# Two tiles' transposes moved up among the products, by 6 and 7 matmul pairs, one evacuation on VectorE during the Gelu table load, one norm behind the first products

## Chip, cores, metric

The kernel runs on one core of a Trainium2 chip. The metric is device time in microseconds (us) of one execution.

## The reference, cut to what matters

Input `x` is 2048 x 448 in bf16. It is layer-normed once, and the result `xn` feeds an attention branch and a gated feed-forward branch:

```python
xn = _layernorm(x, axis=-1)
s  = attention(xn, k_cache, v_cache, wq, wo)                    # 16 heads, window of 512 keys
g  = silu((gelu(xn @ w_gate) * (xn @ w_up)) @ w_down)           # F = 1792
return x + s * g
```

Only the first 14 us matter here: the layer norm of the first four tiles of 128 rows (tiles 0 to 3), their transposition to `xnT`, and the first products `xn @ w_gate`, `xn @ w_up`.

## The kernel before

A tile is normalized on VectorE (`ln_first`: statistics, then a square root on ScalarE; `ln_second`: reciprocal, then the norm itself). For tiles 0 to 3, TensorE (PE) transposes it into a PSUM bank pair (`ln_tp_pe`, "T0" to "T3"), and ScalarE copies ("evacuates") it to `xnT`. Later tiles are transposed by DMA. In the traces each engine's operations appear in the order of the program (ScalarE's before, for instance: the evacuations of T1, T2 and T3 at 7.54, 9.36 and 10.65 us, then the table load at 11.27).

```python
def ln_tp_pe(t, parts):
    ...
            K.op("pe", fn, ...)                      # 8 transposes of 64x128 into PSUM
    for i, b in parts:
        ...
        act(xnT[:, ks, t * P:(t + 1) * P]..., tp[:, ks, :, :], ACT.Copy, b_ps[b:b + 2], ...)   # ScalarE

def warm(n, b):                                      # n matmuls of 256 columns on zeros
    ...
```

`gu_group(units, banks, (a, b), phases)` issues the products of several output units with columns of tiles a to b. It goes through the units in passes: phase 0 has 4 pairs of 64-row matmuls per unit, phase 1 has 3 pairs. One pass over the HEAD, three units, is 12 or 9 pairs. `(0, 0)` and `(0, 1)` are the two halves of phase 0, 6 pairs each over the HEAD. The head of the program, in order:

```python
warm(20, 2)
ln_first(0); ln_first(1); ln_second(0)
ln_tp_pe(0, ((0, 6), (1, 4)))
warm(3, 2)
ln_second(1, "act")
HEAD, PH = (0, 1, 2), (0, 2, 4)
T = ((None, 6),)
ln_first(2)
gu_group(HEAD, PH, (0, 1), ((0, 0), (0, 1)))         # products with T0
ln_tp_pe(1, T)
ln_first(3); ln_second(2); ln_second(3)
ln_a(); ln_a(); ln_b(); ln_b()                       # statistics, then norms, of tiles 4 and 5
gu_group(HEAD, PH, (0, 1), (1,))
gu_group(HEAD, PH, (1, 2), (0,))                     # products with T1
gu_group(HEAD[:1], PH[:1], (1, 2), (1,))
ln_tp_pe(2, T)
gu_group(HEAD[1:], PH[1:], (1, 2), (1,))
gu_group(HEAD[:1], PH[:1], (2, 3), (0,))             # products with T2
ln_tp_pe(3, T)
act(tmp[:, 1, 0:1], nhalf[:, :], ACT.Gelu_apprx_tanh, ...)   # makes ScalarE load the Gelu table
gu_group(HEAD[1:], PH[1:], (2, 3), (0,))
gu_group(HEAD, PH, (2, 3), (1,))
gu_group(HEAD[:2], PH[:2], (3, 4))                   # products with T3
for ph in range(2):
    gu_group((3,), (6,), None, (ph,))                # first products of 512 columns
    gu_group(HEAD[2:], PH[2:], (3, 4), (ph,))
```

These loads of weights and of `x` are all issued from the start on, on SyncE's queue, without waiting for any other operation:

```python
load_x("sp", 4, 2)
for i in (1, 2):                                     # second and third block of w_gate, w_up
    load_w("sp", i, 0); load_w("sp", i, 1); load_wr("sp", i, 0); load_wr("sp", i, 1)
load_x("sp", 6, 2)
load_w("sp", 3, 0); load_w("sp", 3, 1)               # fourth block
load_x("sp", 8, 4)
```

The softmax here doesn't subtract the row's maximum and nothing guards it: scores larger than these inputs give would overflow.

## Time and profile before

| | kernel before |
|---|---|
| time, median of the first 3 runs | 557.43 us (557.25 to 557.52) |
| span of the profiled execution | 555.7 us |
| PE busy in it | 550.3 us |
| head, 0 to 13.4 us: PE busy | 11.58 us |

From the page of the profile before, the busy time of the engines and the chain that ended last:

```profile
span 555.7 us, 9787 instructions
...
PE 550.3 (99%) x3653; PEld 260.6 (47%) x3653; DVE 317.2 (57%) x816; ACT 274.4 (49%) x728; POOL 32.7 (6%) x64
...
PE 98%; DMA 1%; ACT 0%; DVE 0%; issue 0%
```

PE is the bound: it is busy for 99% of the span and makes up 98% of the chain. From the windows view of the same kernel (busy us of each engine in a stretch, instructions in brackets):

```profile
core 0: us, PE busy (x) PEld busy (x) DVE busy (x) ACT busy (x) POOL busy (x), PEclk, DMA share, GB/s
0.00:13.40 13.40, 11.58 (x225) 8.77 (x225) 8.41 (x31) 7.15 (x16) 2.24 (x10) 1.00 0.92 298
13.40:60.00 46.60, 46.60 (x398) 21.60 (x394) 31.15 (x70) 16.74 (x29) 8.87 (x22) 1.00 0.44 90
60.00:545.00 485.00, 484.83 (x2969) 224.82 (x2966) 274.84 (x711) 250.52 (x684) 21.57 (x33) 1.00 0.47 101
```

PE has nothing to lose from 13.4 us on (46.60 of 46.60), and 1.8 us idle before that. From PE's timeline of the kernel before (start, duration, line, operation, output and inputs, count, idle time before it and what ended it):

```profile
5.56 0.40 PE L420 MATMUL bank<-ident,xn 64*128 64x64 bf16 x8
...
7.22 0.28 PE L420 MATMUL bank<-ident,xn 64*128 64x64 bf16 x8
...
8.19 0.34 PE L327 MATMUL bank<-xnT,wgu 64*128 64x128 bf16 x6 [0.19 <-ACT xnT L321]
...
9.04 0.28 PE L420 MATMUL bank<-ident,xn 64*128 64x64 bf16 x8
...
10.10 0.34 PE L327 MATMUL bank<-xnT,wgu 64*128 64x128 bf16 x6 [0.45 <-ACT xnT L321]
...
10.32 0.30 PE L420 MATMUL bank<-ident,xn 64*128 64x64 bf16 x8
...
13.16 0.35 PE L327 MATMUL bank<-xnT,wgu 64*128 64x128 bf16 x6
13.33 0.24 PE L327 MATMUL bank<-xnT,wgur 64*128 64x128 bf16 x2
```

T1's transposes start at 7.22, and T1's first products at 8.19 wait for ScalarE. T2's start at 9.04, and its products at 10.10 wait again. An idle time in brackets counts from the modelled end of the matmul before; counted from start to start, less the 56 ns that a pair of 128-column matmuls takes, the two stalls are 0.35 and 0.61 us. ScalarE's timeline of the kernel before shows why:

```profile
7.54 0.60 ACT L321 ACTIVATE xnT<-bank 128x512 bf16<-128x512 bf16 x1 [0.46 <-PE bank L420]
...
9.36 0.60 ACT L321 ACTIVATE xnT<-bank 128x512 bf16<-128x512 bf16 x1 [1.04 <-PE bank L420]
10.65 0.60 ACT L321 ACTIVATE xnT<-bank 128x512 bf16<-128x512 bf16 x1 [0.70 <-PE bank L420]
11.27 1.28 ACT L321 ACT_TABLE_LOAD   x1
...
12.67 1.06 ACT L321 ACTIVATE gl<-bank 128x512 bf16<-128x512 f32 x2
```

These are the evacuations of T1, T2 and T3, the Gelu table load, and the first Gelu. PE waits for the ends of the first two. The table load comes only after all three.

### The profile page before, as it was taken

What the parts mean: (1) busy time and instruction counts of PE and PEld (TensorE: products, weight loads), DVE (VectorE), ACT (ScalarE), POOL (GpSimd) and SP (SyncE); (2) the same over time, 40 slices, a digit from 0 to 9 for tenths busy, and PEclk for the clock granted to TensorE, in tenths of its full rate; (3) what the DMA queues carried; (4) which work ended last, traced back from release to release, by engine and by line L of the source; (5) the groups of instructions that cost most, each with busy time, mean ns of one, the idle gap of its engine ahead of it and who ended that gap; (6) DMA issues with size and microseconds to landing.
All of it is one profiled execution on the core that took longest, in us unless ns stands there. A gap on an engine that the chain in (4) does not pass through costs nothing.

```text
span 555.7 us, 9787 instructions
## 1 busy us (share of the span) xinstructions
PE 550.3 (99%) x3653; PEld 260.6 (47%) x3653; DVE 317.2 (57%) x816; ACT 274.4 (49%) x728; POOL 32.7 (6%) x64
## 2 busy tenths in 40 slices
PE   8999999999999999999999999999999999999997
PEld 6444444444544444454444445544444454444455
DVE  6783534443385786515858753286785525858722
ACT  5432324353485784504758751085784504758600
POOL 1120830000000000000000000000000000000000
PEclk9999999999999999999999999999999999999999
DMA  9660799403175374313706703176364313807701
GB/s 300 105 164 9 204 292 313 71 1 39 38 132 98 76 139 91 76 35 89 153 20 152 152 20 75 34 140 105 77 151 77 77 34 90 153 20 152 153 8 34
DMA packets 163599, 57.63 MB, mean 104 GB/s; under 512 B 151456, under 2 KB 160672, under 8 KB 163552
## 3 DMA queue, kind: packets, MB, share of 16 engines
q1 hardware_dynamic: 159488, 45.16, 39.6%
q0 software_dynamic: 3296, 11.27, 6.4%
q8 instruction: 29, 0.48, 0.4%
q10 hardware_dynamic: 768, 0.57, 0.3%
q14 instruction: 18, 0.15, 0.1%
HBM read 17.92 MB, written 1.84 MB: 36 GB/s over the span
## 4 chain that ended last, share of the span: by engine, by line
PE 98%; DMA 1%; ACT 0%; DVE 0%; issue 0%
PE bank L327 97%; PE bank L435 1%; DMA pT<-pn 1%; ACT xnT L321 0%; PE bank L420 0%; DVE tmp L668 0%; DVE ofin L671 0%; DVE gl L357 0%; DVE epst L358 0%
## 5 line engine op out<-in xcount | busy, mean ns | idle before, releaser
L629 ACT ACTIVATE p<-bank 128x512 f32<-128x512 f32 x256 | 149.4, 597 | 102.4 <-PE bank L327 102.0
L633 DVE TENSOR_SCALAR pn<-p,rden 128x512 bf16<-128x512 f32 x256 | 124.4, 486 | 16.7 <-DMA pT<-pn 7.9
L327 PE MATMUL bank<-kT,qT 128*128 128x512 bf16 x512 | 121.0, 379 | 0.0
L327 PE MATMUL bank<-pT,va 128*128 128x512 bf16 x512 | 120.8, 379 | 0.2 <-DMA pT<-pn 0.2
L327 PE MATMUL bank<-wo,oT 128*128 128x448 bf16 (+2 forms) x544 | 97.8, 341 | 0.0
L327 PE MATMUL bank<-xnT,wq 64*128 64x512 bf16 x768 | 94.7, 376 | 0.0
L327 PE MATMUL bank<-xnT,wgu 64*128 64x512 bf16 (+1 forms) x780 | 83.4, 347 | 0.6 <-ACT xnT L321 0.6
L327 PEld LDWEIGHTS bank<-pT,va 128*128 128x128 bf16 x512 | 50.0, 98 | 60.8 <-DMA pT<-pn 0.8
L327 PEld LDWEIGHTS bank<-kT,qT 128*128 128x128 bf16 x512 | 49.4, 98 | 61.7 <-issue 3.4
L327 PEld LDWEIGHTS bank<-wo,oT 128*128 128x128 bf16 x544 | 52.0, 98 | 45.5
L615 DVE CAST qT<-bank 128x512 bf16<-128x512 f32 x64 | 42.9, 692 | 48.7 <-PE bank L327 48.7
L321 ACT ACTIVATE qT<-bank 128x512 bf16<-128x512 f32 x64 | 38.2, 597 | 62.1 <-PE bank L327 60.5
L327 PEld LDWEIGHTS bank<-xnT,wq 64*128 64x128 bf16 x768 | 36.8, 94 | 46.8 <-ACT p L629 2.5
L484 DVE TENSOR_TENSOR actT<-bank,gl 128x512 bf16<-128x512 f32 x56 | 37.8, 690 | 34.0 <-PE bank L327 26.7
L321 ACT ACTIVATE gl<-bank 128x512 bf16<-128x512 f32 x56 | 33.2, 597 | 48.0 <-PE bank L327 44.8
L327 PEld LDWEIGHTS bank<-xnT,wgu 64*128 64x128 bf16 x780 | 35.3, 94 | 39.0 <-issue 0.7
L632 DVE RECIPROCAL rden<-rsum 128x1 f32<-128x1 f32 x256 | 40.4, 158 | 22.0 <-ACT p L629 22.0
L629 ACT ACTIVATION_READ_ACCUMULATOR p<-bank 128x1 f32 x256 | 52.8, 206 | 0.0
L668 DVE SCALAR_TENSOR_TENSOR tmp<-bank,g 128x448 f32<-128x448 f32 (+2 forms) x17 | 10.1, 597 | 72.5 <-PE bank L327 72.5
L652 DVE CAST oT<-bank 128x512 bf16<-128x512 f32 x64 | 43.8, 684 | 6.9 <-PE bank L327 6.9
L327 PE MATMUL bank<-wd,actT 128*128 128x448 bf16 x224 | 43.0, 353 | 0.0
L321 ACT ACTIVATE oT<-bank 128x512 bf16<-128x512 f32 x64 | 39.2, 613 | 7.0 <-PE bank L327 7.0
(38 smaller groups left out, 185.1 us busy)
## 6 DMA issues: line engine op xcount, KB each, us to landing
wo<-in_A_wo_dram POOLq DMA_DIRECT2D x4, 896.0 KB, 18.0
wq<-in_A_wq_dram POOLq DMA_DIRECT2D x2, 1536.0 KB, 9.7
va<-in_A_v_cache_dram POOLq DMA_DIRECT2D x8, 256.0 KB, 12.7
pT<-pn SPq DMA_TRANSPOSE x128, 2.8
xr<-in_A_x_dram POOLq DMA_DIRECT2D x16, 112.0 KB, 2.3
out_dram<-ofin SPq DMA_DIRECT2D x15, 112.0 KB, 1.7
wd<-in_B_w_down_dram SPq DMA_DIRECT2D x1, 1568.0 KB, 7.3
x<-in_A_x_dram SPq DMA_DIRECT2D x2, 448.0 KB, 6.7
```

The lines of the kernel that those rows point to most:

```text
L321: K.op("act", lambda e, o=o, i=i: e.activation(o, i, func, scale=scale), reads, writes)
L327: ins = e.matmul(o, lhsT=l, rhs=r, start=st, stop=sp)
L435: ins = e.matmul(bank[b][:, 0:256], lhsT=gl[:, 0, 0:P], rhs=gl[:, 0, 0:256], start=True, stop=True)
L484: K.op("dve", lambda e: e.tensor_tensor(actT[:, c % 2, f, :], bank[b + 1], gl[:, s, :], ALU.mult), (b_ps[b + 1], b_gl[s]), (b_actT[c % 2][ ...
L615: K.op("dve", lambda v, s=s, b=b: v.tensor_copy(qT[:, s, 1, :], bank[b + 1]), (b_ps[b + 1],), (b_qT[s][1],))
L629: K.op("act", lambda e, b=b, r=r, z=z: e.activation(p32[:, z, :], bank[b], ACT.Exp, scale=att_scale, accum_out=rsum[:, r:r + 1]), (b_ps[b] ...
L632: K.op("dve", lambda e, r=r: e.reciprocal(rden[:, r:r + 1], rsum[:, r:r + 1]), (b_rsum[r],), (b_rden[r],))
L633: K.op("dve", lambda e, r=r, z=z, y=y, t=t4 % 2: e.tensor_scalar(pn[:, y, t, :], p32[:, z, :], rden[:, r:r + 1], None, op0=ALU.mult), (b_p ...
L652: K.op("dve", lambda v, i=i, b=b: v.tensor_copy(oT[:, i, :], bank[b]), (b_ps[b],), (b_oT[i],))
L668: K.op("dve", lambda e: e.scalar_tensor_tensor(out=tmp[:, s, c0:c1], in0=bank[b][:, c0:c1], scalar=0.5, in1=g2[:, t, c0:c1], op0=ALU.mult, ...
```

## The change

The intent, as I read the edit: put T1's and T2's transposes earlier among the products (by 6 and 7 pairs) so that their evacuations are done in time; load the Gelu table right after T2's evacuation, with VectorE evacuating T3 meanwhile; take the norm of tile 5 off VectorE's path to the first Gelu products; and drop two warm-up matmuls.

```diff
--- before.py
+++ after.py
@@ -371,9 +371,15 @@
         load_x("sp", 8, 4)
 
 
+        def ln_bn(t):
+            K.op("dve", lambda e: e.bn_stats(stats[:, t, :], x4[:, t, :]), (b_x4[t],), (b_stats[t],))
+
+        def ln_aggr(t):
+            K.op("dve", lambda e: e.bn_aggr(mv[:, t, :], stats[:, t, :]), (b_stats[t],), (b_mv[t],))
+
         def ln_stats(t):
-            K.op("dve", lambda e: e.bn_stats(stats[:, t, :], x4[:, t, :]), (b_x4[t],), (b_stats[t],))
-            K.op("dve", lambda e: e.bn_aggr(mv[:, t, :], stats[:, t, :]), (b_stats[t],), (b_mv[t],))
+            ln_bn(t)
+            ln_aggr(t)
 
         def ln_rstd_pool(t):
             K.op("pool", lambda e: e.tensor_scalar(
@@ -405,7 +411,7 @@
             s = t % NXN
             dma_t(xnT[:, :, t * P:(t + 1) * P], xn[:, s, :], b_xn[s], b_xnT[t])
 
-        def ln_tp_pe(t, parts):
+        def ln_tp_pe(t, parts, eng="act"):
 
             s = t % NXN
             for i, b in parts:
@@ -423,8 +429,12 @@
             for i, b in parts:
                 tp = pall[b // 2].bitcast(BF16)[:, :].rearrange("p (b k c) -> p k b c", b=2, c=R)
                 ks = {None: slice(0, NK + 1), 0: slice(1, 3), 1: slice(0, 4, 3)}[i]
-                act(xnT[:, ks, t * P:(t + 1) * P].rearrange("p k (b c) -> p k b c", c=R), tp[:, ks, :, :],
-                    ACT.Copy, b_ps[b:b + 2], b_xnT[t] if i is None else b_xnT[t][i:i + 1])
+                o = xnT[:, ks, t * P:(t + 1) * P].rearrange("p k (b c) -> p k b c", c=R)
+                bx = b_xnT[t] if i is None else b_xnT[t][i:i + 1]
+                if eng == "act":
+                    act(o, tp[:, ks, :, :], ACT.Copy, b_ps[b:b + 2], bx)
+                else:
+                    K.op("dve", lambda e, o=o, i=tp[:, ks, :, :]: e.tensor_copy(o, i), b_ps[b:b + 2], bx)
 
         last_row = {}
 
@@ -518,34 +528,35 @@
                 ln_tp_dma(ln_t[1])
                 ln_t[1] += 1
 
-        warm(20, 2)
+        warm(19, 2)
         ln_first(0)
         ln_first(1)
         ln_second(0)
         ln_tp_pe(0, ((0, 6), (1, 4)))
-        warm(3, 2)
+        warm(2, 2)
         ln_second(1, "act")
         HEAD, PH = (0, 1, 2), (0, 2, 4)
         T = ((None, 6),)
         ln_first(2)
-        gu_group(HEAD, PH, (0, 1), ((0, 0), (0, 1)))
+        gu_group(HEAD, PH, (0, 1), ((0, 0),))
         ln_tp_pe(1, T)
-        ln_first(3)
+        gu_group(HEAD, PH, (0, 1), ((0, 1), 1))
+        ln_bn(3)
         ln_second(2)
+        ln_aggr(3)
+        ln_std_act(3)
         ln_second(3)
+        gu_group(HEAD[:2], PH[:2], (1, 2), (0,))
+        ln_tp_pe(2, T)
+        gu_group(HEAD[2:], PH[2:], (1, 2), (0,))
+        gu_group(HEAD, PH, (1, 2), (1,))
+
+        act(tmp[:, 1, 0:1], nhalf[:, :], ACT.Gelu_apprx_tanh, (b_nhalf,), (b_tmp[1][0],))
+        gu_group(HEAD[:1], PH[:1], (2, 3), (0,))
         ln_a()
+        ln_tp_pe(3, T, "dve")
         ln_a()
         ln_b()
-        ln_b()
-        gu_group(HEAD, PH, (0, 1), (1,))
-        gu_group(HEAD, PH, (1, 2), (0,))
-        gu_group(HEAD[:1], PH[:1], (1, 2), (1,))
-        ln_tp_pe(2, T)
-        gu_group(HEAD[1:], PH[1:], (1, 2), (1,))
-        gu_group(HEAD[:1], PH[:1], (2, 3), (0,))
-        ln_tp_pe(3, T)
-
-        act(tmp[:, 1, 0:1], nhalf[:, :], ACT.Gelu_apprx_tanh, (b_nhalf,), (b_tmp[1][0],))
         gu_group(HEAD[1:], PH[1:], (2, 3), (0,))
         gu_group(HEAD, PH, (2, 3), (1,))
         gu_group(HEAD[:2], PH[:2], (3, 4))
```

## The prediction

> **What bounds the kernel.** TensorE. The page gives PE 550.3 of 555.7 us busy, and the chain of waits is 98% PE. The windows view shows PE busy 46.60 of 46.60 us from 13.4 to 60 us and 484.83 of 485.00 from 60 to 545, at full granted clock. Only the head is loose: 11.58 of 13.40 us. The change touches only the head; the question is how many tenths of a microsecond of stall go, and whether all later matmuls start earlier by as much.
>
> **Stalls in the head** (starts of matmuls in the timeline, less the 56 ns of a 128-column pair): 0.35 us before T1's first products (8.19, waiting for ScalarE's evacuation of T1, 7.54 to 8.14) and 0.61 us before T2's (10.10; evacuation 9.36 to 9.96). T3 is evacuated 10.65 to 11.25, in time for its products at 11.40. T0's transposes go out at 5.557 although the first part of norm 0 ended at 5.28: the 20th cold warm-up matmul (213 ns each) streamed until 5.42. Products start at 6.52 after three more warm-ups.
>
> **What the change does.** It adds no PE work; two warm-ups go. T3's evacuation moves from ScalarE (0.60 us) to VectorE. No bf16 PSUM copy on VectorE is in this trace; a float one of 128x512 takes 0.68 us[...].
>
> Reconstruction, with the trace's durations:
> - T0's first transposes at about 5.34, products at about 6.28 (was 6.52): -0.24.
> - T1's transposes at about 6.6 (7.22), evacuation from 7.07, behind the standard deviation of tile 2; T1 products about 7.7 (8.19). Stall left about 0.14.
> - Tile 2 normalized at about 8.07 (8.17). T2's transposes at 8.2 (9.04), evacuation 8.53 to 9.13 behind tile 3's standard deviation; T2 products about 9.2 (10.10). Stall left 0.15 to 0.2.
> - Tile 3 normalized later, about 9.4 (9.16), as its aggregate and square root wait for norm 2. T3's transposes at about 9.45; VectorE first does tile 4's statistics (to 10.2)[...].
> - The Gelu table load starts at about 9.1 instead of 11.27. Before, it set the first Gelu (12.67); now the matmuls do. Tile 5's norm has about 10 us to spare.
>
> Sum: stalls of 0.96 + 0.24 go, 0.35 to 0.7 come back: the first 512-column products are 0.5 to 0.8 us earlier (12.30 before, about 11.6 expected). As PE is gapless afterwards, this should reach the end.
>
> **Predicted time:** 556.8 us (557.43 before), 80% range 556.3 to 557.3. Faster by over 2%: 0.5%; within 2%: 99%; slower by over 2%: 0.5%.
>
> **What would show it:** first 512-column products near 11.6; stalls under 0.25 us before T1's and T2's products; a wait on VectorE before T3's; no wait of PE between 12 and 60 us.
>
> **What would make it wrong:** [...] here spacing went from 213 ns to full speed at about 6.3 us. [...] Also a slow VectorE copy, weights landing late, or a transpose wait in attention that swallows the gain.

Its sum came to 0.5 to 0.8 us: stalls of 0.96 + 0.24 go, and 0.35 to 0.7 come back. Of what comes back, 0.29 to 0.34 are the stalls left before T1's and T2's products; the rest was a new stall before T3's. Of the last paragraph the first fear is that two warm-ups fewer would delay full matmul speed.

## The result, and the profile after

The changed kernel measured 557.40 us (median of 6; 556.87 to 558.08), the kernel before in the same rounds 557.47 (557.25 to 558.12). The ratio is 0.9996, with a 95% interval from 0.9983 to 1.0009: unchanged within noise. (A ratio is the mean time of one kernel's runs over that of the other's of the same rounds, so it is not quite the ratio of the medians quoted.) The predicted class is right and the median lies 0.1 us above the predicted range.

The page of the changed kernel, the same lines as before:

```profile
span 555.1 us, 9781 instructions
...
PE 549.7 (99%) x3651; PEld 260.1 (47%) x3651; DVE 317.0 (57%) x817; ACT 273.9 (49%) x727; POOL 32.9 (6%) x64
...
PE 98%; DVE 0%; DMA 0%; issue 0%
```

The span of this execution is 0.6 us shorter, almost exactly as predicted, but not for the predicted reasons. The windows view of the changed kernel:

```profile
0.00:13.40 13.40, 11.32 (x227) 8.53 (x229) 9.30 (x31) 7.01 (x15) 2.38 (x10) 1.00 0.91 299
13.40:60.00 46.60, 46.60 (x396) 21.45 (x392) 30.74 (x70) 16.40 (x28) 9.27 (x22) 1.00 0.41 90
60.00:545.00 485.00, 485.00 (x2970) 225.04 (x2965) 274.14 (x711) 250.54 (x684) 21.25 (x33) 1.00 0.48 101
```

PE's busy time in the head even fell. PE's timeline of the changed kernel shows where the gain came and where it went:

```profile
5.38 0.44 PE L426 MATMUL bank<-ident,xn 64*128 64x64 bf16 x8 [0.50 <-DVE xn L401]
...
6.60 0.29 PE L426 MATMUL bank<-ident,xn 64*128 64x64 bf16 x8
...
8.17 0.28 PE L426 MATMUL bank<-ident,xn 64*128 64x64 bf16 x8
...
9.46 0.30 PE L426 MATMUL bank<-ident,xn 64*128 64x64 bf16 x8
...
12.29 0.29 PE L327 MATMUL bank<-xnT,wgu 64*128 64x128 bf16 x4
12.92 0.23 PE L327 MATMUL bank<-xnT,wgu 64*128 64x128 bf16 x2 [0.34 <-issue]
```

T1's transposes are at 6.60 instead of 7.22, T2's at 8.17 instead of 9.04. T1's and T2's products now wait 0.11 and 0.22 us (from start to start) where they had waited 0.35 and 0.61. But the last two lines are new: PE starts four matmuls at 12.29, the last at 12.37, and the next at 12.92, in the middle of a run of equal instructions. The view calls this "issue": nothing that it knows of was awaited. The weight load that ends the pause carries no semaphore wait in the trace. In the kernel before, this place (13.16 to 13.33 in the timeline shown there) has no pause. ScalarE's and VectorE's timelines of the changed kernel:

```profile
7.08 0.58 ACT L321 ACTIVATE xnT<-bank 128x512 bf16<-128x512 bf16 x1
...
8.49 0.60 ACT L321 ACTIVATE xnT<-bank 128x512 bf16<-128x512 bf16 x1
9.11 1.28 ACT L321 ACT_TABLE_LOAD   x1
...
11.37 1.08 ACT L321 ACTIVATE gl<-bank 128x512 bf16<-128x512 f32 x2 [0.76 <-PE bank L327]
```

```profile
9.88 0.18 DVE L378 BATCH_NORM_AGGREGATE mv<-stats 128x2 f32<-128x6 f32 x1
9.98 0.39 DVE L437 COPY xnT<-bank 128x512 bf16<-128x512 bf16 x1
...
12.08 1.29 DVE L494 TENSOR_TENSOR actT<-bank,gl 128x512 bf16<-128x512 f32 x2 [0.40 <-ACT gl L321]
```

ScalarE's lines are the evacuations of T1 and T2, the table load, now at 9.11 instead of 11.27 (1.28 us; the next activation starts at 10.40), and the first Gelu. VectorE's COPY is T3's evacuation: 0.39 us, where ScalarE took 0.60.

Landmarks of PE, in us:

| PE reaches | before | after | predicted |
|---|---|---|---|
| T0's transposes | 5.56 | 5.38 | 5.34 |
| first products | 6.52 | 6.09 | 6.28 |
| T1's transposes / products | 7.22 / 8.19 | 6.60 / 7.72 | 6.6 / 7.7 |
| T2's transposes / products | 9.04 / 10.10 | 8.17 / 9.24 | 8.2 / 9.2 |
| T3's transposes / products | 10.32 / 11.40 | 9.46 / 10.53 | 9.45 / - |
| first products of 512 columns | 12.30 | 11.44 | 11.6 |
| first 512-column pair behind the run in which the pause lies | 13.40 | 13.05 | no pause |

To compare whole traces I lined up the weight loads of the two by order, counted from the end, and took the difference of their starts. The changed kernel leads by 0.87 us at 11.4 us, and by 0.37 us from 13 us on. The lead grows to 0.72 us at 210 us only because the profiled execution of the kernel before waited there for a DMA transpose in the attention, and ends at 0.61 us. Such waits come and go between executions: r1_again (below) loses 0.36 us at 378 us, c2_defer_t3act 0.33 us at 163 us, and r3_wide has one at 210 us too. So I do not credit this part to the change.

So the question is what PE waits for at 12.37 us.

**Theory A.** PE ran out of instructions. The DMA view lists a queue of kind "instruction" with 29 packets (q8); each moves 16 KB. PE recorded about 7450 instructions, which is 257 for each packet. In the changed kernel such a packet starts at 10.46 us and ends at 11.60, while the queues are full of weight loads. (A second queue of this kind, q14, moves 8 KB at a time; in the run it has nothing before 24 us.) What PE does when a packet comes late no view shows directly; the experiments below test the theory.

**Rivals.** B: a one-off of that execution. C: the two kernels are simply equal. D: a pause at a fixed place or time, unconnected with the queues. E: held-back loads help by themselves.

### The profile page after: what moved, and what is told of

The parts are those of the page before. It is cut to its first block, busy times and chain, and to the rows that moved or that the text cites. A ratio compares the mean times of both kernels' runs of the same rounds, so it can differ in the third digit from the quotient of the medians.

```text
span 555.1 us, 9781 instructions
## 1 busy us (share of the span) xinstructions
PE 549.7 (99%) x3651; PEld 260.1 (47%) x3651; DVE 317.0 (57%) x817; ACT 273.9 (49%) x727; POOL 32.9 (6%) x64
## 3 DMA queue, kind: packets, MB, share of 16 engines
q0 software_dynamic: 3296, 11.27, 6.9%
## 4 chain that ended last, share of the span: by engine, by line
PE 98%; DVE 0%; DMA 0%; issue 0%
PE bank L327 98%; DMA x<-in_A_x_dram 0%; DVE stats L375 0%; PE bank L426 0%; DVE xn L401 0%; DVE mv L378 0%; PE bank L445 0%; DVE tmp L679 0%; DVE ofin L682 0%; DVE rstd L395 0%
## 6 DMA issues: line engine op xcount, KB each, us to landing
wq<-in_A_wq_dram POOLq DMA_DIRECT2D x2, 1536.0 KB, 11.4
```

## The experiments

Times are medians; every kernel gave the correct result. Kernels of one job share the runs of the kernel before, whose median was 557.48, 557.28 and 557.27 in the three jobs.

### r1_again: the changed kernel once more

No edit.

> The changed kernel once more, unchanged. In its first profile PE was 0.86 us ahead of the kernel before at 12.4 us and then stood still for 0.5 us (12.37 to 12.92) in front of a weight load that carries no semaphore wait. Theory A (PE ran out of fetched instructions; the 16 KB instruction packet started at 10.46 us, behind the weight loads): the stall comes again within a few matmuls of the same place, PE resumes at 12.7 to 13.2, and the time is 0.1 to 0.5 us under the kernel before in the mean. Rival B (a one-off of that execution): no stall, 0.8 us under the kernel before. Rival C (the kernels are equal and the spread of 1 us hides nothing): ratio 1.000.

Measured: 556.55 us, ratio 0.9982 (0.9969 to 0.9996). The pause is there again, between the same two matmuls: 12.31 to 12.92 us, 0.56 us beyond normal spacing. In the view of PE's waits of this run it is

```profile
PE bank L327 <- issue: 0.4, 1, 0.4
```

B falls. The five runs are in two clusters, 556.27 to 556.55 and 557.20 to 557.25, and the profiled one is in the upper; the profile cannot say whether the lower ones had the pause. The time itself was better than I expected from A, and better than in the first measurement. The two together (11 runs) have a mean of 557.10, the 15 runs of the kernel before in the same rounds 557.65. So C is unlikely, but the times alone do not exclude it: the first measurement agrees with it.

### r2_defer: loads that are not yet needed are held back

```diff
-        for i in (1, 2): ...            # third block, fourth block, x 6 to 11: at the start
+        def late_loads():
+            gate = (b_xnT[2][0],)       # T2 evacuated
+            load_w("sp", 2, 0, gate)
+            load_w("sp", 2, 1); load_wr("sp", 2, 0); load_wr("sp", 2, 1)
+            load_x("sp", 6, 2); load_w("sp", 3, 0); load_w("sp", 3, 1); load_x("sp", 8, 4)
...
         ln_tp_pe(2, T)
+        late_loads()
```

> The changed kernel with the loads of the third and fourth weight blocks and of x tiles 6 to 11 held back until T2 is evacuated (about 9.1 us), so that the DMA queues are nearly empty from 8 to 10 us. Theory A: the instruction packet starts well before 10.4 us, the PE stall at 12.4 us is gone or under 0.1 us, PE is 0.8 us ahead of the kernel before from there on, and the time falls to about 556.6 (ratio 0.9985). Rival B/D (the pause is not tied to the DMA queues): stall of 0.5 us as before and ratio 0.9995. If the held-back weights come late, a wait on DMA appears at 15 to 21 us instead.

Measured: 556.61 us (556.23 to 556.72), ratio 0.9981 (0.9969 to 0.9994). The DMA view from 7.5 to 11.5 us (busy share in tenths, a slice is 0.1 us; then the instruction queue), first the changed kernel, then this one:

```profile
DMA  9999999999999999999999999999999999999999
...
q8 instruction: 1, 0.02, 1.8%
```

```profile
DMA  9999875421000060000000000000949628699999
...
q8 instruction: 1, 0.02, 1.7%
```

In the changed kernel the packet lies somewhere in a solid wall of nines (it starts at 10.46 us). Here the queues run empty, and the packet starts at 8.91 us, almost alone. PE's timeline of this kernel at the place in question:

```profile
12.51 0.35 PE L327 MATMUL bank<-xnT,wgu 64*128 64x128 bf16 x6
12.68 0.24 PE L327 MATMUL bank<-xnT,wgur 64*128 64x128 bf16 x2
12.75 1.21 PE L327 MATMUL bank<-xnT,wgu 64*128 64x512 bf16 x14
```

Six matmuls of the run go on without a break where the changed kernel broke off after four. The pause is gone, no DMA wait took its place, and PE keeps its lead, here 0.65 us (0.8 was expected). This is what A said. In time, this kernel and r1_again of the same rounds can't be told apart (means 556.56 and 556.73).

### r3_wide and r4_split: fewer and more instructions ahead, with the same warm-up time

```diff
-        warm(19, 2) ... warm(2, 2)                      # matmuls of 256 columns
+        warm([512] * 9 + [256], 2) ... warm([512], 2)   # r3_wide:  20 instructions fewer
+        warm([128] * 38, 2) ... warm([128] * 4, 2)      # r4_split: 42 instructions more
```

> The changed kernel with the same warm-up time in fewer instructions: nine 512-column and one 256-column matmul for the nineteen of 256, one of 512 for the two. That is 11 matmuls and 11 weight loads fewer ahead of the products minus none elsewhere, 20 instructions in all. Theory A (a boundary at a fixed instruction count, fetched at a fixed time): the boundary lies 10 matmuls later in the products, and PE gets there about 0.5 us later as five 512-column pairs lie between, so the stall shrinks to 0 to 0.2 us; time about 556.8. Rival D (stall at a fixed place of the program or a fixed time): stall of 0.5 us at the same matmul.

> The changed kernel with the same warm-up time in more instructions: thirty-eight 128-column matmuls for nineteen of 256, four for two: 42 instructions more ahead of the products. Theory A: the boundary lies 21 matmuls earlier in the products, reached near 11.2 us, and PE stands there until the instructions are there: a stall of 1 us or more (if they still arrive at about 12.9), less by what an earlier request of the packet gives back; time 0.2 to 0.8 us over the changed kernel. Rival D: stall unchanged in place and size.

(r3_wide has 10 matmuls and 10 weight loads fewer; the 11 of the expectation are a slip.) Measured: r3_wide 556.70 us, ratio 0.9987 (0.9975 to 1.0000), no pause. This is weaker evidence than it looks, as PE came late for another reason; its waits from 5 to 30 us in r3_wide:

```profile
PE bank L327 <- DMA wgu<-in_B_w_up_dram: 0.6, 1, 0.6
```

Its first products waited for weights, and its lead was only 0.50 us when it reached the count of instructions described below, 2.69 us after the start of its packet.

r4_split 558.02 us, ratio 1.0006 (0.9994 to 1.0019): 0.6 us over the first measurement of the changed kernel and 1.5 us over r1_again, where 0.2 to 0.8 was expected. PE's timeline of r4_split:

```profile
10.97 0.29 PE L327 MATMUL bank<-xnT,wgu 64*128 64x128 bf16 x4
12.70 0.64 PE L327 MATMUL bank<-xnT,wgu 64*128 64x128 bf16 x10 [1.45 <-issue]
```

The pause came 1.3 us earlier (behind a matmul at 11.03 instead of 12.31) and was three times as long: 1.61 us beyond normal spacing. Counted in weight loads from the start, it lies behind the 219th in the changed kernel and in r1_again, and behind the 220th here, although 21 more warm-ups stand in front. Counted in everything that the trace records on PE, waits included, it lies behind the 449th instruction in all three. It is fixed to a count of instructions and not to a place in the program or a time. D falls. PE resumed 2.46, 2.61 and 2.66 us after the start of the packet (changed kernel, r1_again, r4_split).

### c1_before_defer and f1_before_defer2: is it the loads alone?

The same held-back loads in the kernel before, first put after `ln_tp_pe(2, T)`, then after `ln_tp_pe(1, T)` with T1 as the gate.

> Control: the kernel before, with only the late weight and x loads held back until T2 is evacuated (10.0 us there). It has no instruction stall to lose. Theory A: same time as the kernel before, ratio 0.9995 to 1.0005, PE positions unchanged within 0.1 us up to 13 us; so what the held-back kernel gained (ratio 0.9981) is the change's own gain set free, not a gain of the loads. Rival E (held-back loads help by themselves, for instance by less DMA traffic during the norms): ratio 0.9985 or lower.

Measured: 563.12 us, ratio 1.0102. My edit was bad. In the kernel before, the DMA transposes of tiles 4 and 5 stand ahead of `ln_tp_pe(2, T)` in the program, so on SyncE's queue they stood ahead of the held-back loads, which left at 15.39 us instead of about 10. PE's waits of this kernel from 5 to 30 us:

```profile
core 0 of [0], span 562.9 us
engine line waited for: us in total, times, longest us
PE bank L327 <- DMA wgur<-in_B_w_up_dram: 3.7, 1, 3.7
PE bank L327 <- ACT xnT L321: 0.6, 2, 0.4
```

PE waited 3.7 us for weights, and its granted clock, 1.00 from 10 to 20 us, was 0.54 from 20 to 24 us. This run says nothing about rival E, only that these held-back loads, queued behind two transposes that waited until 11.66 us, left too late.

> The control again, mended: in the first one the held-back loads stood in SyncE's queue behind two transposes and came 6 us late, which was my edit's fault. Here they are queued ahead of the transposes and released by T1's evacuation (8.1 us). Theory A: ratio 0.9995 to 1.0005 of the kernel before, PE positions unchanged within 0.1 us at 13 us, no DMA wait at 17 us; the gain of the held-back changed kernel is then the change's own. Rival E (the held-back loads help by themselves): ratio 0.9985.

Measured: 557.25 us, ratio 0.9999 (0.9987 to 1.0012). PE leads the kernel before by 0.15 us in the profile, which it already has at the first products (6.33 against 6.52); the two stalls of 0.35 and 0.61 us are unchanged. E falls: holding back the loads is worth nothing to the kernel before that these runs can resolve. What r2_defer gained belongs to the change.

### c3_split_defer and c4_wide_defer: both edits together

> Both edits together: 42 more warm-up instructions and held-back loads. The split warm-ups alone stalled PE 1.66 us at 11.03 us. Theory A: the request comes 42 instructions earlier than in the held-back kernel (packet there at 8.91 us) or at about the same time, and no backlog delays it, so the packet starts at 7.9 to 9.0 us; PE resumed 2.5 to 2.7 us after the packet's start in three traces, so it is served by 10.5 to 11.6: stall 0 to 0.5 us instead of 1.66, time 556.6 to 557.1. Rival (more instructions cost by themselves, about 1 us): time stays near 558.0.

Measured: 556.59 us, ratio 0.9985 (0.9973 to 0.9996). The packet starts at 8.14 us, and the pause of 1.6 us behind the 220th load is gone. A delay of 0.15 us is left, eight loads later, at the first 512-column products; I have not explained it. Forty-two more instructions cost r4_split 1.5 us over r1_again of its job (558.02 against 556.55), and cost nothing that these runs can resolve when their packet is not held up (c3_split_defer 556.59, c4_wide_defer 556.40).

> Both cures together: wide warm-ups (20 instructions fewer) and held-back loads. Theory A: either cure alone removes the stall, so together they give nothing more: 556.5 to 556.8, no stall at 12 to 13.5 us. If each removed a separate cost: about 556.0.

Measured: 556.40 us (556.20 to 556.78), ratio 0.9983 (0.9971 to 0.9995), no pause. The two cures do not add up, as A said. This has the lowest median, about 1 us under the kernel before, but r1_again, r2_defer and c3_split_defer are not distinguishable from it.

### What each part of the change is worth: c2, f2, f3, c5

These four undo one part each on r2_defer, where no pause hides the effect.

```diff
-        ln_tp_pe(3, T, "dve")                           # c2_defer_t3act
+        ln_tp_pe(3, T)
```

> The changed kernel with held-back loads, but T3 evacuated by ScalarE again, in the order that the change left: behind the Gelu table load (9.1 to 10.4 us). If VectorE's copy is needed as its title says: T3's evacuation runs at about 10.6 to 11.2, PE waits 0.4 to 0.7 us before T3's products near 10.7, and the time rises by 0.4 to 0.6 us over the same kernel with the copy on VectorE (556.6), to about 557.1. If the copy's engine does not matter: no wait and 556.6.

Measured: 557.38 us, ratio 1.0002, against 0.9983 and 0.9985 of c4 and c3 in the same job. ScalarE's timeline of c2_defer_t3act:

```profile
9.05 1.28 ACT L321 ACT_TABLE_LOAD   x1
10.35 0.20 ACT L321 ACTIVATE tmp<-nhalf 128x1 f32<-128x1 f32 x1
10.45 0.58 ACT L321 ACTIVATE xnT<-bank 128x512 bf16<-128x512 bf16 x1
```

The evacuation of T3 (10.45) had to wait until the table was loaded, and PE's lead fell from 0.92 to 0.22 us at T3's products. So the copy on VectorE is worth 0.7 us on PE, given that the table load has moved up. In time, the mean is 0.93 and 1.02 us above those of c3 and c4, more than the 0.4 to 0.6 that I had expected.

```diff
         ln_b()
+        ln_b()                                          # f2_defer_norm5
```

> The changed kernel with held-back loads, but the norm of tile 5 ahead of the first Gelu product again. VectorE's next norm waits for GpSimd's reciprocal root (about 12.3), so the norm ends near 12.9 and the product of unit 0 starts there instead of at 12.29 (its end 13.6 instead of 13.0); PE wants the two banks of unit 0 at about 13.5 (11.65 plus 1.9). Expected: PE wait of 0.1 to 0.3 us near 13.5, time 0.1 to 0.3 over 556.55. If the move of this norm buys nothing: no wait.

Measured: 556.81 us, ratio 0.9992 (0.9978 to 1.0005). VectorE's timeline of f2_defer_norm5 shows tile 5's norm and the first Gelu product:

```profile
12.46 0.61 DVE L407 TENSOR_SCALAR xn<-x,mv,rstd 128x448 bf16<-128x448 bf16 x2 [0.64 <-POOL rstd L393]
12.98 0.69 DVE L500 TENSOR_TENSOR actT<-bank,gl 128x512 bf16<-128x512 f32 x1
```

The product starts at 12.98 instead of 12.29 (r2_defer), and PE loses 0.22 us at 13.5 us. This is as expected, though too small for the time to show by itself.

```diff
-        gu_group(HEAD, PH, (0, 1), ((0, 0),))           # f3_defer_t12back: T1, T2 where they were
-        ln_tp_pe(1, T)
-        gu_group(HEAD, PH, (0, 1), ((0, 1), 1))
+        gu_group(HEAD, PH, (0, 1), ((0, 0), (0, 1)))
+        ln_tp_pe(1, T)
+        gu_group(HEAD, PH, (0, 1), (1,))
...                                                      # and T2 behind one pass and one unit more
```

> The changed kernel with held-back loads, but T1's and T2's transposes back at their old places among the products. Expected from the durations: T1's transposes 0.34 us later, T1's products wait about 0.3 us (0.04 now); T2's transposes behind one more unit and one more pass, T2's products wait 0.5 us (0.22 now). First 512-column products 0.5 to 0.7 us later than 11.4 to 11.65; time 557.0 to 557.3, that is, most of the gain gone. If the places do not matter: 556.55.

Measured: 557.04 us (mean 557.23), ratio 0.9998 (0.9985 to 1.0010). PE's waits of this kernel from 5 to 30 us:

```profile
PE bank L327 <- ACT xnT L321: 0.6, 2, 0.4
```

These are the two stalls of the kernel before, again of 0.35 and 0.61 us from start to start, and the whole lead is gone. So the places of T1's and T2's transposes are needed for the gain, as T3's copy on VectorE is (c2_defer_t3act); each of the two, undone alone, costs about 0.7 us of PE's lead.

```diff
-        warm(19, 2) ... warm(2, 2)
+        warm(20, 2) ... warm(3, 2)                      # c5_defer_warm23
```

> The changed kernel with held-back loads, but 20 and 3 warm-up matmuls again instead of 19 and 2. Expected: T0's transposes at 5.37 to 5.55, products 0 to 0.25 us later, depending on when the full clock comes in that execution; time 0 to 0.2 us over 556.55, likely inside the noise. If fewer warm-ups cost something by delaying the full clock: time 0.1 us or more under 556.55.

Measured: 556.85 us, ratio 0.9990 (0.9977 to 1.0002). T0's transposes went out at 5.56 as in the kernel before; f2 and f3 of the same job had them at 5.35 and 5.38. Products started at 6.64 against 6.27 and 6.36, and the lead was 0.56 us against f2's 0.72. In time this is inside the noise. In these traces fewer warm-ups did not delay full matmul speed: the last half-rate matmul came at 6.7 us here, with 23 warm-ups, and with 21 at 6.8 us in f3_defer_t12back and before 4.2 us in the changed kernel. (What the expectation calls the full clock is read from the spacing of 256-column warm-ups, in the changed kernel 213 ns, then 109; the granted clock was 1.00 throughout, from 1.18 to 8 us.)

### When the packet leaves

In the eight kernels whose held-back loads worked, the queues were nearly empty and the first instruction packet started when PE had begun between 117 and 125 weight loads (about 250 recorded instructions). c3_split_defer, with 21 more loads in front, is among them (118), so the packet follows PE's count and not the time or the place; from this I infer that q8 brings PE's instructions. With full queues it started after 145 (before), 179 (after), 176 (r1_again), 164 (r3_wide) and 186 loads (r4_split). Taking the 122nd load as the time of the request, an estimate, the packet was held up by 1.2 us in the kernel before and by 1.7 us in the changed one. In the kernel before it started at 10.38 us. With the 2.46 to 2.66 us from packet to resumption, the next instructions were there at 12.84 to 13.04 us, an estimate, and PE came for them (the load behind the 219th) at 13.17. The kernel before had only 0.1 to 0.3 us in hand. That is roughly what the changed kernel could keep of its lead.

## Why the prediction was right or wrong

- **Bound, stalls, sizes: right.** The head's 0.35 and 0.61 us of stall, and the time of T0's transposes, were what there was to win. After the change 0.11 and 0.22 are left (0.14 and 0.15 to 0.2 predicted), and T1's and T2's products came within 0.05 us of the reconstruction. f3_defer_t12back shows that these stalls go with the two transposes' places.
- **T3's copy: no wait, to the good.** The prediction expected PE to wait for VectorE before T3's products. The copy took 0.39 us (392 ns), ended at 10.37, and PE, whose T3 products started at 10.53, did not wait for it.
- **Lead at the first 512-column products: 0.87 us where 0.5 to 0.8 was predicted.** It varies between executions: 0.93 us in r1_again, the same program, and 0.65 us in r2_defer, whose head is the same up to there but for the loads. Two dates that the change does not set differ between the traces. One is the start of full matmul speed: in the profiled execution of the kernel before the warm-ups ran at half rate to the end (213 ns), in that of the changed kernel full speed (109 ns) came at 4.1 us. It cannot be all, as r1_again had its first 19 warm-ups as slow as the kernel before. The other is the landing of the first weights: in r2_defer the last transfer of the first `w_up` block landed at 6.28 us (5.36 in the changed kernel), and its first products started at 6.42 instead of 6.09. I take 0.65 to 0.95 us for the change's own lead, an estimate from these traces.
- **"As PE is gapless afterwards, this should reach the end": this step failed.** The kernel before was gapless because, by the estimate above, PE came just late enough for its instructions. When it came 0.87 us earlier, it stood still for 0.5 us at a fixed count of instructions, in theory A until the next packet of instructions was there, and the lead fell to 0.37 us. r1_again repeated the pause, r4_split moved and tripled it by adding instructions, r2_defer and c4_wide_defer removed it, and f1_before_defer2 showed that the loads alone bring nothing that can be resolved. The gain did not leave the critical path; it turned into a wait that the list of what could go wrong did not have.
- **Fewer warm-ups: the feared loss did not come.** The last half-rate matmul was as late with 23 warm-ups (6.7 us, c5_defer_warm23) as with 21 (6.8 us, f3_defer_t12back), and in that of the changed kernel, also with 21, it was before 4.2 us. Full speed came anywhere from 4.1 to 6.8 us, and at 4.1 and 5.8 us in two executions of the same program (the changed kernel and r1_again). What sets its time these traces do not show.
- **Still open.** The two executions of the changed kernel whose traces are on record had the pause; whether the others had it each time, and how long, can't be seen. PE resumed 1.3 to 1.5 us after the end of the packet (11.60 to 12.92 us in the changed kernel), not at its end; what happens in between these traces do not show. The two measurements of the changed kernel (0.9996 and 0.9982) differ within their intervals, and the better one has runs as fast as the kernels without a pause, so its size may vary from run to run. That held-back loads make the changed kernel faster is shown in the traces, not in the times; that a late packet costs time is shown in the times too, by r4_split against c3_split_defer (ratios 1.0006 and 0.9985).

## What to carry to other kernels

Before counting a stall's removal as gained, ask what else the engine takes from memory and how much later than needed it could still come: here the instruction packet of a stretch of small matmuls (64 rows, 128 columns, 28 ns each) shared the DMA engines with weight loads (it started at 10.46 us in full queues, at 8.91 in nearly empty ones), and a lead of 0.87 us met a margin of a few tenths. Where the view says "issue" in the middle of equal instructions, count instructions from the start, and add or drop some in front: a pause that stays at a count, as here, points to the instructions themselves. Loads that are not needed yet can be held back to let such packets through, as in r2_defer; but look at what stands ahead of them in their queue: in c1_before_defer they stood behind two waiting transposes, left at 15.39 us instead of about 10, and PE waited 3.7 us.
